# Low parts of the first product's weights and of the first q: VectorE in place of GpSimd

## The chip, the cores and the metric

The kernel runs on one core of a Trainium2 chip. The metric is the time of one execution on the device in microseconds (us). Five engines take part: TensorE (PE, with PEld for its weight loads), VectorE (DVE), ScalarE (ACT), GpSimd (POOL) and SyncE (SP), which issues most of the transfers.

## The reference

An attention with mixing across heads, and behind it two feed-forward blocks:

```
scores = einsum('bhij,hg->bgij', (q @ k^T) / sqrt(64), w_pre)
attn   = einsum('bhij,hg->bgij', softmax(scores), w_post)
x      = (attn @ v), heads side by side           # 1792 tokens x 768
x      = ((x @ w1) * (x @ w2)) @ w3 @ w_out       # 768 -> 1024 -> 1024 -> 768
out    = relu(x @ w_in)^2 @ w_out2                # 768 -> 2048 -> 768
```

There are 4 batches, 12 heads, 448 positions and a head width of 64. The weights arrive as 64-bit floats, two 32-bit words an element.

## The kernel before, in words

`w3 @ w_out` doesn't depend on x, so the kernel forms it first, once (`Prod34`): this is the first product. To multiply in 32-bit precision, each operand is split into a high part, in the reduced format that TensorE takes, and a low part, the difference to it; three matmuls (high-high, high-low, low-high) stand for one product (`mm3`, line 53).

The weights pass through `Weights` in 33 pieces: piece 0 and piece 2 are 256 columns wide, 16 pieces of w_out are 384 wide, and 15 pieces of w3 are 512 wide (7 of them in the first half, pieces 5, 8, ... 23; the last 8, pieces 25 to 32, belong to the second half). A piece goes through these steps:

- load on SyncE's queue into one of five `raw` buffers (line 68);
- `narrow` on ScalarE (line 80), which makes `y` from the upper words;
- `join` parts 0, 1, 2 on VectorE (lines 92, 94, 96), which put the 32-bit float `f` together;
- `high` on ScalarE (line 110), which writes the high part from `f`;
- `rest` on GpSimd (line 114), which writes the low part, `f` minus the high part.

The order on each engine is the order of the program, written by hand: nothing is reordered. `Prod34.stage(s)` issues, one after the other, the load of piece s+6, the narrow of s+4, then on VectorE join 1 of s+2, join 0 of s+3, join 2 of s+2, then the high part of s+2, and last the low part of s+1. `half0` runs 25 stages, with the matmuls of each stage's piece behind it, evacuates its sums (lines 194 and 195, columns split between ScalarE and VectorE) with two more stages between, and `half1` runs the remaining stages with the second half of the product.

Between the stages `prologue(i)` puts in the work that the attention needs first, by the table `PRO`: the loads of k and q of batch 0, the high part of q (`high_q`, line 313, on ScalarE for the first chunk n = 0) and its low part (`low_q`, line 318, on GpSimd for every n), the high parts of k (line 289, ScalarE) and their low parts (`low_k`, line 296, on VectorE for batch 0), the first score matmuls (`scores`, line 335) and their evacuation (`evac`, line 342, ScalarE). The score sums have two buffers. Chunk 0 has three groups of q, each of 480 columns and four heads; their steps are `split_q` at i = 5, 8 and 13. From i = 15 the steps of the attention proper are mixed in, and the feed-forward blocks follow, whose weights go through the same `Weights` class with its own stage order.

Of the kernel before, what the change touches and what calls it, by code (L numbers as in the profile page):

```python
# [14 lines left out]
ALU = mybir.AluOpType  # L15
# [18 lines left out]
def fused_kernel(ctx, tc, q, k, v, w_pre, w_post, w1, w2, w3t, wo, win, wo2, eye, out):  # L34
    nc = tc.nc
# [10 lines left out]
    def f32(ap):  # L46
        return ap.bitcast(F)
# [9 lines left out]
    class Weights:  # L57
# [51 lines left out]
        def high(self, i):  # L109
            nc.scalar.activation(self.out[i][0], self.ft[i], AF.Copy)  # L110

        def rest(self, i):
            if i in self.ft:
                nc.gpsimd.tensor_tensor(self.out[i][1], self.ft.pop(i), f32(self.out[i][0]), ALU.subtract)  # L114

    HC = DM // 2

    class Prod34:
# [29 lines left out]
        def stage(self, s):  # L148
            w = self.w
            ok = lambda i: 0 <= i < len(self.seq)  # L150
            if ok(s + 6):
                k, c, x, lo, hi, _ = self.seq[s + 6]
                src, n = (wo, HC) if k == "o" else (w3t, PW)
                w.load(s + 6, src[c, :, n * x + lo : n * x + hi], True)
            if ok(s + 4):
                w.narrow(s + 4)
            if ok(s + 2) and s > 0:
                w.join(s + 2, 1)
            if ok(s + 3):
                w.join(s + 3, 0)  # L160
                if s < 0:
                    w.join(s + 3, 1)
                    w.join(s + 3, 2)
            if ok(s + 2):
                if s >= 0:
                    if s == 0:
                        w.join(s + 2, 1)
                    w.join(s + 2, 2)
                k, c, x, lo, hi, _ = self.seq[s + 2]
                w.place(s + 2, tuple(t[:, lo:hi] for t in self.tile(k, c, x)))  # L170
                w.high(s + 2)
            if ok(s + 1):
                w.rest(s + 1)

        def product(self, acc, m, h, cs):
            for c in cs:
# [64 lines left out]
    class Attention:  # L241
# [73 lines left out]
        def low_q(self, n, g4):  # L315
            tl = self.ka.tile([128, 4 * IC], R, tag="ql", name=f"ql{n}_{g4}", bufs=3)
            tl = self.ql[n, g4] = tl[:, : 4 * CHUNKS[n % 4][1]]
            nc.gpsimd.tensor_tensor(tl, self.qraw.pop((n, g4)), f32(self.qh[n, g4]), ALU.subtract)

        def split_q(self, n, g4):  # L320
            self.high_q(n, g4)
# [558 lines left out]
```

## Time and profile before

| | |
|---|---|
| median of 3 runs | 1411.32 us (1411.06 to 1411.37) |
| the profiled execution | 1411.11 us, of which the span from first to last instruction 1409.2 us |
| TensorE busy in the span | 1375.7 us (98%) |
| VectorE, ScalarE, GpSimd busy | 771.5 us (55%), 643.0 us (46%), 509.5 us (36%) |
| mean granted TensorE clock | 0.994 of full speed |

The span is that of the trace; the time of the execution has 1.9 us around it. The shares are means over stages of different kinds: the first product and the prologue take the first 90 us or so, the attention and the feed-forward blocks the rest.

### The profile page before, as it was taken

The page shows a single profiled execution, that of the slowest core. Times are in us where ns is not written, and L with a number is a line of the kernel's source. Part 1 is how long each engine was busy: PE and PEld are TensorE (multiplying, and loading weights), DVE is VectorE, ACT ScalarE, POOL GpSimd, SP SyncE. Part 2 cuts the span into 40 slices and gives each one's busy share as a digit, 9 for nine tenths or more (in the row PEclk, how much of TensorE's full clock was granted, in tenths as well). Part 3 has the DMA queues.
Part 4 walks back from the last instruction along what each step waited for, and adds up shares of the span by engine and source line. Part 5 has one row for each costly group of instructions (what it writes and reads, how often), then busy time and mean ns, then how long its engine had stood idle before and what let it go on. Part 6 is the DMA issues. An engine that isn't in the chain of part 4 may idle for free.

```text
span 1409.2 us, 22743 instructions
## 1 busy us (share of the span) xinstructions
PE 1375.7 (98%) x8136; PEld 1191.6 (85%) x8136; DVE 771.5 (55%) x1320; ACT 643.0 (46%) x1394; POOL 509.5 (36%) x604
## 2 busy tenths in 40 slices
PE   6789999999999999999999999999999999999998
PEld 5678777777777777899999999999999999999998
DVE  8963444443444444645317963985454227944972
ACT  4456655666656655433323533543333224533530
POOL 4543563563455335322222322234222222222231
PEclk9899999999999999999999999999999999999999
DMA  7774463444455325533223442355443123433441
GB/s 217 226 229 149 151 186 127 154 165 151 148 165 161 127 97 170 154 107 101 64 61 101 125 124 78 106 179 185 117 112 104 53 79 101 128 109 80 126 140 59
DMA packets 95509, 183.69 MB, mean 130 GB/s; under 512 B 20581, under 2 KB 62053, under 8 KB 94949
## 3 DMA queue, kind: packets, MB, share of 16 engines
q1 hardware_dynamic: 89861, 178.82, 41.2%
q10 hardware_dynamic: 5536, 3.42, 0.8%
q8 instruction: 65, 1.06, 0.3%
q14 instruction: 47, 0.39, 0.1%
HBM read 129.52 MB, written 14.16 MB: 102 GB/s over the span
## 4 chain that ended last, share of the span: by engine, by line
PE 93%; DVE 3%; issue 2%; ACT 1%; DMA 1%; ACTq 0%; DVEq 0%
PE l L53 50%; PE sp L357 11%; PE tp L406 11%; PE y L53 8%; PE pv L448 6%; PE sc L335 5%; PE q L53 1%; DVE f L92 1%; DVE f L94 1%; DVE f L96 1%; PE e L53 1%; DMA kraw<-k 0%; DMA raw<-w3t 0%; ACT kt L289 0%; ACT y L80 0%
## 5 line engine op out<-in xcount | busy, mean ns | idle before, releaser
L114 POOL TENSOR_TENSOR wl<-f,wh 128x384 fp32r<-128x384 f32 (+1 forms) x176 | 196.1, 1118 | 501.4 <-ACT wh L110 480.8
L363 DVE TENSOR_REDUCE nm<-sp 120x1 f32<-120x448 f32 x180 | 112.3, 624 | 208.5 <-PE sp L357 205.8
L92 DVE TENSOR_SCALAR f<-y 128x384 int32<-128x384 int32 (+2 forms) x209 | 147.0, 703 | 88.1 <-POOL wl L114 83.1
L406 PEld LDWEIGHTS tp<-kwr,p 120*112 120x112 f32 (+1 forms) x1440 | 173.5, 176 | 24.6 <-issue 13.7
L406 PE MATMUL tp<-kwr,p 120*112 120x120 f32 (+1 forms) x1440 | 176.9, 266 | 0.0
L357 PE MATMUL sp<-r,kpre 120*120 120x448 f32 x360 | 173.4, 563 | 0.0
L342 ACT ACTIVATE s<-sc 120x448 f32<-120x448 f32 (+1 forms) x192 | 99.3, 542 | 108.6 <-PE sc L335 107.7
L96 DVE SCALAR_TENSOR_TENSOR f<-raw,f 128x384 int32<-128x384 int32 (+2 forms) x209 | 142.0, 679 | 6.1
L396 POOL TENSOR_SCALAR kwr<-kw,sm 120x120 f32<-120x120 f32 x180 | 106.6, 599 | 104.6 <-DVE sm L391 68.2
L94 DVE SCALAR_TENSOR_TENSOR f<-y,f 128x384 int32<-128x384 int32 (+2 forms) x209 | 139.4, 667 | 6.2
L53 PE MATMUL l<-bhh,wh 128*128 128x448 f32 x384 | 141.3, 368 | 0.0
L53 PE MATMUL l<-blh,wh 128*128 128x448 f32 x384 | 141.1, 368 | 0.0
L53 PE MATMUL l<-bhh,wl 128*128 128x448 f32 x384 | 139.4, 363 | 0.0
L110 ACT ACTIVATE wh<-f 128x384 fp32r<-128x384 f32 (+1 forms) x176 | 96.4, 548 | 85.1 <-DVE f L96 79.5
L371 ACT ACTIVATE p<-sp,nm 120x448 f32<-120x448 f32 x180 | 113.5, 631 | 30.4 <-PE tp L406 24.4
L335 PE MATMUL sc<-kt,qh 128*120 128x448 f32 (+1 forms) x192 | 119.1, 620 | 5.0 <-DVE kt L296 2.8
L80 ACT ACTIVATE y<-raw 128x384 f32<-128x384 f32 (+2 forms) x209 | 120.6, 577 | 7.3 <-DMA raw<-w3t 2.9
L448 PE MATMUL pv<-p,v 112*64 112x120 f32 (+1 forms) x1536 | 94.6, 266 | 0.8 <-DVE p L421 0.8
L724 ACT ACTIVATE r<-l 128x448 f32<-128x448 f32 x64 | 34.9, 546 | 116.6 <-PE l L53 116.6
L448 PEld LDWEIGHTS pv<-p,v 112*64 112x64 f32 x1536 | 74.2, 136 | 12.7 <-issue 1.2
L421 DVE COPY p<-tp 112x480 f32<-112x480 f32 (+1 forms) x90 | 58.9, 655 | 45.5 <-PE tp L406 45.3
L53 PEld LDWEIGHTS l<-bhh,wh 128*128 128x128 f32 x384 | 71.8, 187 | 7.2
(104 smaller groups left out, 2837.8 us busy)
## 6 DMA issues: line engine op xcount, KB each, us to landing
r<-s SPq DMA_DIRECT2D x172, 210.0 KB
raw<-w SPq DMA_DIRECT2D x64, 384.0 KB
raw<-win SPq DMA_DIRECT2D x64, 384.0 KB
raw<-wo SPq DMA_DIRECT2D x48, 512.0 KB
kraw<-k SPq DMA_DIRECT2D x24, 448.0 KB
qraw<-q SPq DMA_DIRECT2D x36, 240.0 KB
raw<-w3t SPq DMA_DIRECT2D x15, 512.0 KB
raw<-wo SPq DMA_DIRECT2D x16, 384.0 KB
```

The lines of the kernel that those rows point to most:

```text
L53: nc.tensor.matmul(acc, w, x, start=(first and i == 0 and j == 0), stop=(last and i == n - 1 and j == 2))
L80: nc.scalar.activation(y, self.raw[i][:, :, 1].bitcast(F), AF.Copy, scale=2.0**-112)
L92: nc.vector.tensor_scalar(fi, yi, 3, 0x7FFFFFFF, ALU.logical_shift_left, ALU.bitwise_and)
L94: nc.vector.scalar_tensor_tensor(fi, yi, -0x80000000, fi, ALU.bitwise_and, ALU.bitwise_or)
L96: nc.vector.scalar_tensor_tensor(fi, raw[:, :, 0], 29, fi, ALU.logical_shift_right, ALU.bitwise_or)
L114: nc.gpsimd.tensor_tensor(self.out[i][1], self.ft.pop(i), f32(self.out[i][0]), ALU.subtract)
L335: nc.tensor.matmul(sc[:ic], t[:, hh * ic : hh * ic + ic], self.kt[b, h // 2][:, h % 2], start=(i == 0), stop=(i == 1))
L357: nc.tensor.matmul(t[:kk], self.kpre[:kk, :kk], self.rt.pop(g)[:kk], start=True, stop=True)
L363: nc.vector.tensor_reduce(nm[:kk], self.sp[g][:kk], AX.X, ALU.max, negate=True)
L371: nc.scalar.activation(p[:kk], self.sp.pop(g)[:kk], AF.Exp, bias=self.nm.pop(g)[:kk], accum_out=self.sm[g // 2][:kk, g % 2 : g % 2 + 1],)
L406: nc.tensor.matmul(t[:, j, :, :cnt], p[:kk, j * JP : j * JP + JP], w[:kk, :, :cnt], start=True, stop=True)
L448: nc.tensor.matmul(t[64 * e : 64 * e + 64], self.v[b][:, j, g], self.p2[n][:, j, g, :ic], start=(j == 0), stop=(j == JC - 1),)
```

## The change

The low parts of all 33 pieces of the first product's weights, and the low parts of q in chunk 0, are computed on VectorE. In the stage the low part of piece s+1 is now issued ahead of the joins, where it was last. The feed-forward blocks keep GpSimd for theirs, as do the later q chunks.

```diff
-        def rest(self, i):
+        def rest(self, i, eng=nc.gpsimd):
             if i in self.ft:
-                nc.gpsimd.tensor_tensor(self.out[i][1], self.ft.pop(i), f32(self.out[i][0]), ALU.subtract)
+                eng.tensor_tensor(self.out[i][1], self.ft.pop(i), f32(self.out[i][0]), ALU.subtract)
...
             if ok(s + 4):
                 w.narrow(s + 4)
+            if ok(s + 1):
+                w.rest(s + 1, nc.vector)
             if ok(s + 2) and s > 0:
                 w.join(s + 2, 1)
...
                 w.high(s + 2)
-            if ok(s + 1):
-                w.rest(s + 1)
...
-            nc.gpsimd.tensor_tensor(tl, self.qraw.pop((n, g4)), f32(self.qh[n, g4]), ALU.subtract)
+            eng = nc.gpsimd if n else nc.vector
+            eng.tensor_tensor(tl, self.qraw.pop((n, g4)), f32(self.qh[n, g4]), ALU.subtract)
```

## Rows read from the trace of the kernel before

**Rows 1.** Page, first part: busy us of each engine, share, instructions.

```profile
PE 1375.7 (98%) x8136; PEld 1191.6 (85%) x8136; DVE 771.5 (55%) x1320; ACT 643.0 (46%) x1394; POOL 509.5 (36%) x604
```

**Rows 2.** Windows of three stretches: length; busy PE, PEld, DVE, ACT, POOL; clock; DMA.

```profile
0.00:50.00 50.00, 33.01 (x138) 29.57 (x139) 44.92 (x66) 23.36 (x44) 24.29 (x24) 0.90 0.73 217
50.00:91.00 41.00, 30.41 (x142) 26.97 (x141) 40.44 (x52) 23.79 (x42) 22.13 (x15) 0.91 0.78 253
91.00:1409.00 1318.00, 1312.32 (x7860) 1135.10 (x7858) 686.12 (x1204) 595.85 (x1309) 463.04 (x565) 1.00 0.40 123
```

**Rows 3.** Groups by shape, first 150 us: the joins; busy, mean ns, idle before.

```profile
L96 DVE SCALAR_TENSOR_TENSOR f<-raw,f 128x512 int32<-128x512 int32 x15 | 17.3, 1151 | 0.0
...
L94 DVE SCALAR_TENSOR_TENSOR f<-y,f 128x512 int32<-128x512 int32 x15 | 15.0, 1001 | 0.1
L92 DVE TENSOR_SCALAR f<-y 128x512 int32<-128x512 int32 x15 | 14.3, 951 | 0.2 <-ACT y L80 0.2
...
L94 DVE SCALAR_TENSOR_TENSOR f<-y,f 128x384 int32<-128x384 int32 x16 | 13.1, 817 | 0.1
...
L96 DVE SCALAR_TENSOR_TENSOR f<-raw,f 128x384 int32<-128x384 int32 x16 | 13.0, 813 | 0.0
...
L92 DVE TENSOR_SCALAR f<-y 128x384 int32<-128x384 int32 x16 | 6.9, 433 | 0.0
```

**Rows 4.** Timeline, 35 to 42 us: start, duration, engine, line; brackets: idle and releaser.

```profile
35.30 1.49 DVE L96 SCALAR_TENSOR_TENSOR f<-raw,f 128x512 int32<-128x512 int32 x1
...
36.90 0.64 ACT L110 ACTIVATE w3h<-f 128x512 fp32r<-128x512 f32 x1 [1.38 <-DVE f L96]
37.18 0.35 DVE L92 TENSOR_SCALAR f<-y 128x384 int32<-128x384 int32 x1
...
37.45 0.55 DVE L96 SCALAR_TENSOR_TENSOR f<-raw,f 128x384 int32<-128x384 int32 x1
37.61 1.51 POOL L114 TENSOR_TENSOR w3l<-f,w3h 128x512 fp32r<-128x512 f32 x1 [1.38 <-ACT w3h L110]
37.92 1.62 DVE L94 SCALAR_TENSOR_TENSOR f<-y,f 128x384 int32<-128x384 int32 x1
...
40.62 0.55 DVE L96 SCALAR_TENSOR_TENSOR f<-raw,f 128x384 int32<-128x384 int32 x1
...
41.20 0.53 ACT L110 ACTIVATE woh<-f 128x384 fp32r<-128x384 f32 x1 [1.33 <-DVE f L96]
```

**Rows 5.** Timeline, 4 to 88 us: single instructions of DVE, POOL and PE.

```profile
4.80 0.29 DVE L92 TENSOR_SCALAR f<-y 128x256 int32<-128x256 int32 x1 [4.80 <-ACT y L80]
...
48.63 1.49 DVE L96 SCALAR_TENSOR_TENSOR f<-raw,f 128x512 int32<-128x512 int32 x1
...
51.44 1.42 POOL L318 TENSOR_TENSOR ql<-qraw,qh 128x480 fp32r<-128x480 f32 x1 [1.87 <-ACT qh L313]
...
74.17 0.68 DVE L96 SCALAR_TENSOR_TENSOR f<-raw,f 128x512 int32<-128x512 int32 x1
74.77 0.68 DVE L94 SCALAR_TENSOR_TENSOR f<-y,f 128x512 int32<-128x512 int32 x1
75.37 0.41 DVE L92 TENSOR_SCALAR f<-y 128x512 int32<-128x512 int32 x1
75.71 0.68 DVE L96 SCALAR_TENSOR_TENSOR f<-raw,f 128x512 int32<-128x512 int32 x1
...
77.03 1.71 POOL L318 TENSOR_TENSOR ql<-qraw,qh 128x480 fp32r<-128x480 f32 x1 [3.06 <-ACT qh L313]
...
86.05 1.16 DVE L296 TENSOR_TENSOR kt<-kraw,kt 64x448 fp32r<-64x448 f32 x2
...
87.17 0.47 PE L335 MATMUL sc<-kt,qh 128*120 128x448 f32 x1 [0.42 <-ACT s L342]
```

**Rows 6.** Chain that ended last, in order of time: start, duration, what.

```profile
94.58 2.09 PE q L53 x12
```

## The prediction

> **What bounds the kernel now.** The page's first part names TensorE as the bound of the whole, busy 98% of the span [rows 1]. I then cut the span into windows, since a share is a mean. Behind 91 us TensorE is busy 1312.3 of 1318.0 us at a clock of 1.00. Ahead of it, where the changed lines run, VectorE is the full engine: 44.9 of the first 50 us, although its first instruction starts only at 4.80, and 40.4 of the next 41, while TensorE works 33.0 and 30.4 [rows 2, 5]. So the prologue lasts as long as VectorE's queue, and what is added to or taken from that queue up to the point where TensorE takes over moves the end one for one; later there are only 5.7 us of TensorE idle to absorb anything.
>
> That point is in the timeline: the scores of heads 4 and 5 start at 87.17, as the low part of their k, the pair of subtractions at 86.05, ends on VectorE [rows 5]. In the table `PRO` it stands behind stage 31, so behind every changed piece.
>
> Next, what VectorE's time consists of. Groups by shape give the joins means far above their undisturbed durations: the 512-wide join 2 takes 1151 ns in the mean but 0.68 at 75.71 [rows 3, 5]. The timeline says why: the join at 37.92 takes 1.62 us because GpSimd's low part runs from 37.61 to 39.12; the one at 37.45, just ahead of it, takes 0.55 [rows 4]. Whenever GpSimd has started first, the join waits until it has ended.
>
> **What the change removes.** The waiting of joins for GpSimd. By durations (mean minus undisturbed, 0.41, 0.68, 0.68 us for joins 0, 1, 2 at 512 wide [rows 5]; 0.35, 0.55, 0.55 at 384 [rows 4]): 15 × (0.54 + 0.32 + 0.47) + 16 × (0.08 + 0.27 + 0.26) = 29.8 us [rows 3], and about 0.8 for the two narrow pieces, 30.6. By elapsed time, from 4.80 to 87.21, 82.4 us: undisturbed joins follow each other by 0.27 and 0.47 us at 384 wide (37.18, 37.45, 37.92 [rows 4]) and by 0.60, 0.34 and again 0.60 at 512 (from 74.17 on [rows 5]), so 16 × 1.21 + 15 × 1.54 = 42.5; three pairs of k parts at 1.16 are 3.5; four copies, the narrow pieces and the preparation of the mixing weights are some 4.5 (an estimate by width). The rest, 31.9, is waiting. I take 31.0 and keep 30.6 to 31.9.
>
> **What it adds as work.** A 32-bit subtraction from two operands in SBUF is no row of VectorE at these widths; the k parts do just that, 448 wide, in 0.58 each [rows 5], which fits between the joins 1 and 2 at 0.47 (384) and 0.60 (512). So 16 × 0.47 + 15 × 0.60 + 2 × 0.34 = 17.2, and the first two groups of q, 480 wide, 2 × 0.57 = 1.1; the third comes behind the deciding point, where TensorE is the bound. Sum 18.3.
>
> If this were all, VectorE would gain 31.0 - 18.3 = 12.7 us. The Trainium skill's SBUF — State Buffer, section Who interferes with whom, says that GpSimd and a VectorE instruction with two SBUF inputs exclude each other for a whole instruction, the later one blocked. By that alone the sum would be 1411.1 - 12.7 = 1398.4; the trace agrees on the blocking (1.62 against 0.55 [rows 4]).
>
> **What it adds as waiting.** The low part of a piece needs `f` and the high part. In the new order join 2 of a piece is VectorE's last instruction of a stage, ScalarE's high part follows it, and the low part is VectorE's first instruction of the next stage. VectorE executes in order, so it stands still while ScalarE works, and the joins of the next two pieces, the next high part and the load into the freed buffer stand behind it. Before, the same wait was GpSimd's and cost VectorE nothing.
>
> Its price: from the start of join 2 at 384 wide, 0.55 to its end (40.62 to 41.17), 0.03 to ScalarE's start (41.20), 0.53 for the high part, and the hand-over to the next engine, 0.07 from 37.54 to GpSimd's 37.61 [rows 4]: 1.18, where the next join would have come after 0.47. Stall 0.71. At 512 wide: 1.49 until join 2 ends at 36.79 (0.68 undisturbed), 0.11 to 36.90, 0.64, 0.07, together 1.50 against 0.60. Stall 0.90. The hand-over to VectorE itself is bounded by nothing and by twice that, so 0.07 either way a piece; I take the row.
>
> Piece by piece, up to the deciding point:
> - 15 of the 384-wide pieces in full: 15 × 0.71 = 10.7. The first pieces are excepted: their low parts come behind a whole join of another piece. The preparation of the premix weights fills about 0.4 of one stall.
> - Eight 512-wide pieces in full (six of the first half, 25 and 32): 8 × 0.90 = 7.2.
> - Piece 20: the low part of q is issued first and waits for two ScalarE instructions. GpSimd waited for the same pair: join 2 from 48.63, end 50.12, GpSimd at 51.44 [rows 5], so 1.3 + 0.08 = 1.4.
> - Pieces 27 and 28: one copy of 0.47 stands between, 2 × 0.43 = 0.9. Piece 26 has two copies between, 30 and 31 a pair of k parts (1.16): nothing. If those covers were gone, 0.9 each.
> - Piece 29: q's second group waits for the high part, a k conversion and its own high part. Join 2 at 74.17 ends at 74.85, GpSimd started at 77.03 [rows 5]: 2.2 + 0.1 = 2.3.
>
> Sum 10.7 - 0.4 + 7.2 + 1.4 + 0.9 + 2.3 = 22.1 us.
>
> The VectorE page of the Trainium skill (VectorE: DVE Perf Modes, The DRAIN you can't avoid) says that semaphores between chained VectorE instructions cost nothing extra and that the number of instructions counts; this is measured inside one engine, and by it the 22.1 would be nothing and the time again 1398.4. No row here has the round trip over ScalarE on VectorE's queue, only on GpSimd's.
>
> **Costed at nothing.** The loads: a piece's buffer comes free later but stages lengthen by the same, so the lead in stages stays. TensorE: per piece of the first product it has 12 matmuls or none, 2.09 us at full clock [rows 6], two such per three pieces, whose VectorE time becomes (2 × 1.68 + 2.14) + 2 × 0.71 + 0.90 = 7.8. GpSimd is left idle there, and none of its other work starts earlier.
>
> **The sum.** -31.0 + 18.3 + 22.1 = +9.4 us, on the profiled execution's own 1411.1 (span and 1.9 around it; 0.2 under the median of the runs): 1420.5.
>
> **The rivals.**
> 1. *Faster: the round trip is hidden.* If ScalarE's high part were done when VectorE comes to the low part, blocking goes and only 18.3 comes: 1398.4. The turning point is a mean stall of 12.7 / 22.1 = 57% of mine, 0.41 and 0.52 us. Against it: ScalarE's instruction alone takes 0.53 and 0.64 [rows 4]. For it: VectorE's durations hold some tail that may overlap. Chance 0.07.
> 2. *No change: VectorE's delay isn't passed on whole.* TensorE's 5.7 idle us behind 91 [rows 2] could swallow some, leaving 1414.8; with shorter hand-overs too, 1411 to 1414. Against it: nothing suggests that idle waits for anything else than its own stages. Chance of ending within 0.2%: 0.06.
> 3. *Slower still: TensorE drops to its lower clock.* The prologue has 0.90 and 0.91 granted [rows 2]; more idle could put it at the lower of its two levels, 1.2 of 2.4 GHz, where 24 matmuls take 8.4 against VectorE's 7.8: 0.6 a step over seven steps, and 1.5 to 2 in the first TensorE-bound work behind the deciding point, 1426. Chance 0.12.
>
> **How the numbers follow.** The forecast has 0.75. Its own range: the hand-over gives ± 0.07 × 25 = 1.8, the blocking - 0.9 to + 0.4, so 1418 to 1423. The 8-in-10 range leaves out rival 1 and the far ends of 2 and 3: 1414.5 to 1424.5. A measurement of this kernel tells 0.2%, 2.8 us, from no change: slower 0.75 + 0.12 = 0.87, same 0.06, faster 0.07.
>
> **What would show it.** After: the joins' means in the prologue fall to their undisturbed values (512-wide join 0 to about 410 ns); VectorE, not GpSimd, has idle time ahead of line 114, ended by ScalarE's line 110, 0.6 to 0.9 us a piece and about 20 in all; VectorE's busy share of the first 90 us falls while the scores of heads 4 and 5 start near 96.5; from there everything is shifted by a constant. It would be wrong if that idle is under 13 us, or if the scores start late but the end doesn't.

## The result, and the profile after

The changed kernel takes 1419.44 us (median of 4 runs, 1418.92 to 1420.05), the kernel before 1411.28 beside it: a ratio of 1.0059, with a 95% interval of 1.0046 to 1.0072, so slower by 8.2 us. The forecast was 1420.5, with a range of 1414.5 to 1424.5.

The page's first part after the change, to be set beside [rows 1]:

```profile
PE 1376.7 (97%) x8136; PEld 1192.0 (84%) x8136; DVE 760.1 (54%) x1356; ACT 642.8 (45%) x1394; POOL 461.4 (33%) x568
```

36 instructions (33 low parts of weights, 3 of q) moved from GpSimd to VectorE, and yet VectorE is busy 11.4 us less: the time in which a join waited for GpSimd had counted as busy time. The windows over the same stretches as [rows 2], the last one to the end (columns: length; busy PE, PEld, DVE, ACT, POOL; clock; DMA share; GB/s):

```profile
0.00:50.00 50.00, 30.13 (x126) 25.72 (x127) 35.11 (x78) 21.36 (x40) 0.19 (x4) 0.93 0.67 200
50.00:91.00 41.00, 27.01 (x115) 24.20 (x115) 32.72 (x64) 20.83 (x37) 0.00 (x0) 0.84 0.68 222
91.00:1417.00 1326.00, 1319.53 (x7898) 1142.11 (x7896) 692.28 (x1216) 600.60 (x1318) 461.26 (x564) 1.00 0.40 124
```

VectorE went from 44.9 and 40.4 us of work to 35.1 and 32.7, but TensorE got less done in these 91 us, 57.1 us of work against 63.4. The engine that bounds the stretch has become less busy and the stretch longer: what grew is a wait. Groups by shape over the first 150 us show both sides of it (busy us, mean ns, idle before, releaser), the joins beside [rows 3]:

```profile
L114 DVE TENSOR_TENSOR w3l<-f,w3h 128x512 fp32r<-128x512 f32 x15 | 10.3, 690 | 6.0 <-ACT w3h L110 5.9
L96 DVE SCALAR_TENSOR_TENSOR f<-raw,f 128x512 int32<-128x512 int32 x15 | 10.3, 684 | 0.0
L94 DVE SCALAR_TENSOR_TENSOR f<-y,f 128x512 int32<-128x512 int32 x15 | 10.3, 684 | 0.0
...
L114 DVE TENSOR_TENSOR wol<-f,woh 128x384 fp32r<-128x384 f32 x16 | 8.9, 558 | 9.5 <-ACT woh L110 9.5
...
L92 DVE TENSOR_SCALAR f<-y 128x512 int32<-128x512 int32 x15 | 6.3, 420 | 0.0
```

The 512-wide joins fell from 951, 1001 and 1151 ns to 420, 684 and 684. In front of the low parts VectorE stands idle for 15.5 us, and ScalarE's high part ends 15.4 of them. One such wait at either width in the timeline (start, duration, engine, line; in brackets the idle time and what ended it):

```profile
21.41 0.55 DVE L96 SCALAR_TENSOR_TENSOR f<-raw,f 128x384 int32<-128x384 int32 x1
22.00 0.52 ACT L110 ACTIVATE woh<-f 128x384 fp32r<-128x384 f32 x1 [1.43 <-DVE f L96]
...
22.55 0.56 DVE L114 TENSOR_TENSOR wol<-f,woh 128x384 fp32r<-128x384 f32 x1 [0.59 <-ACT woh L110]
...
23.90 0.68 DVE L96 SCALAR_TENSOR_TENSOR f<-raw,f 128x512 int32<-128x512 int32 x1
24.68 0.63 ACT L110 ACTIVATE w3h<-f 128x512 fp32r<-128x512 f32 x1 [1.71 <-DVE f L96]
...
25.34 0.69 DVE L114 TENSOR_TENSOR w3l<-f,w3h 128x512 fp32r<-128x512 f32 x1 [0.76 <-ACT w3h L110]
```

From join 2 to the low part it is 1.14 and 1.44 us. And the place from which TensorE takes over, in the same columns:

```profile
93.62 0.69 DVE L114 TENSOR_TENSOR w3l<-f,w3h 128x512 fp32r<-128x512 f32 x1 [0.70 <-ACT w3h L110]
...
94.35 1.16 DVE L296 TENSOR_TENSOR kt<-kraw,kt 64x448 fp32r<-64x448 f32 x2
95.11 0.44 PE L336 MATMUL sc<-kt,qh 128*120 128x448 f32 x1 [0.32 <-DVE kt L296]
```

The scores of heads 4 and 5 start at 95.11 instead of 87.17 [rows 5], 7.9 us later; the span grew by 1417.1 - 1409.2 = 7.9. What happens behind this point has not changed its length, 1322.0 us in both; in the ten runs below it is 1321.6 to 1323.6 us.

### The profile page after: what moved, and what is told of

It is laid out like the page before. It is cut to its first block, busy times and chain, and to the rows that moved or that the text cites. A ratio compares the mean times of both kernels' runs of the same rounds, so it can differ in the third digit from the quotient of the medians.

```text
span 1417.1 us, 22708 instructions
## 1 busy us (share of the span) xinstructions
PE 1376.7 (97%) x8136; PEld 1192.0 (84%) x8136; DVE 760.1 (54%) x1356; ACT 642.8 (45%) x1394; POOL 461.4 (33%) x568
## 4 chain that ended last, share of the span: by engine, by line
PE 93%; DVE 3%; ACT 1%; issue 1%; DMA 1%; ACTq 0%; SPq 0%; DVEq 0%
PE l L53 50%; PE sp L358 11%; PE tp L407 10%; PE y L53 8%; PE pv L449 6%; PE sc L336 5%; PE q L53 2%; DVE f L94 1%; DVE f L96 1%; PE e L53 1%; ACT w3h L110 1%; ACT woh L110 0%; DVE f L92 0%; PE p L53 0%; DMA raw<-w3t 0%
## 5 line engine op out<-in xcount | busy, mean ns | idle before, releaser
L92 DVE TENSOR_SCALAR f<-y 128x384 int32<-128x384 int32 (+2 forms) x209 | 137.9, 660 | 87.9 <-POOL wl L114 83.1
L94 DVE SCALAR_TENSOR_TENSOR f<-y,f 128x384 int32<-128x384 int32 (+2 forms) x209 | 130.4, 624 | 6.1
L96 DVE SCALAR_TENSOR_TENSOR f<-raw,f 128x384 int32<-128x384 int32 (+2 forms) x209 | 130.0, 622 | 6.1
L319 POOL TENSOR_TENSOR ql<-qraw,qh 128x480 fp32r<-128x480 f32 (+1 forms) x45 | 51.0, 1134 | 109.2 <-DVE qh L311 109.2
```

Source lines behind the costliest of these rows:

```text
L92: nc.vector.tensor_scalar(fi, yi, 3, 0x7FFFFFFF, ALU.logical_shift_left, ALU.bitwise_and)
L94: nc.vector.scalar_tensor_tensor(fi, yi, -0x80000000, fi, ALU.bitwise_and, ALU.bitwise_or)
L96: nc.vector.scalar_tensor_tensor(fi, raw[:, :, 0], 29, fi, ALU.logical_shift_right, ALU.bitwise_or)
```

## The experiments

Ten kernels ran, all times medians beside the kernel before at 1411.3 on the same chip.

**The low parts on VectorE, at the end of the stage.** One block of the changed kernel moves, its operations and engine stay:

```diff
-            if ok(s + 1):
-                w.rest(s + 1, nc.vector)
             if ok(s + 2) and s > 0:
                 w.join(s + 2, 1)
...
                 w.high(s + 2)
+            if ok(s + 1):
+                w.rest(s + 1, nc.vector)
```

> The low parts stay on VectorE, but are issued at the end of the stage, behind join 2 of the next piece, where the high part has long been written. Theory (the loss is VectorE's wait for ScalarE's high part): of the sum's three terms the wait of the weights goes, only the two waits of q stay (1.4 and 2.3 us): -31.0 + 18.3 + 3.7 = -9.0 us against the kernel before, about 1402 us, range 1400 to 1405. Rival (the 33 subtractions themselves are the loss, wherever they stand): unchanged, about 1419 us.

Measured: 1403.99 us, a ratio of 0.9946 (0.9929 to 0.9963). The same 33 subtractions on the same engine are worth -7.3 us at one place of the stage and +8.2 at the other. VectorE's timeline of this run:

```profile
38.20 0.55 DVE L96 SCALAR_TENSOR_TENSOR f<-raw,f 128x384 int32<-128x384 int32 x1
38.67 0.68 DVE L114 TENSOR_TENSOR w3l<-f,w3h 128x512 fp32r<-128x512 f32 x1
39.27 0.55 DVE L94 SCALAR_TENSOR_TENSOR f<-y,f 128x384 int32<-128x384 int32 x1
...
64.42 0.43 DVE L92 TENSOR_SCALAR f<-y 128x512 int32<-128x512 int32 x1 [1.69 <-ACT y L80]
...
69.10 0.66 DVE L319 TENSOR_TENSOR ql<-qraw,qh 128x480 fp32r<-128x480 f32 x1 [3.05 <-ACT qh L313]
...
79.42 1.16 DVE L296 TENSOR_TENSOR kt<-kraw,kt 64x448 fp32r<-64x448 f32 x2
```

No low part of a weight has idle time ahead of it any more. The gain stayed 1.7 us under the 9.0 expected. Most of that is at the rows at 64.42 and 69.10: VectorE, now ahead, meets ScalarE's narrow step and waits longer for q. A smaller part lies at TensorE. Its window from the first scores of heads 0 and 1 to those of heads 4 and 5, in the columns of [rows 2], has no gap:

```profile
72.69:80.73 8.04, 8.04 (x33) 7.75 (x33) 7.75 (x14) 5.16 (x10) 0.00 (x0) 0.71 0.61 181
```

So the place from which TensorE is full has come forward to 72.69, and TensorE starts there at its lower clock, after 9 us without work: four score matmuls and twelve of the product take 1.82 and 3.47 us, the next ones 0.81 and 2.10. The scores of heads 4 and 5 start at 80.73, 0.7 us after the end of the k subtraction that they need (the first of the pair at 79.42, which takes 0.62), where it was 0.1 in the changed kernel.

**Between join 0 and join 2.** The same block behind `w.join(s + 3, 0)`.

> The low parts on VectorE between join 0 and join 2 of the stage: joins 1 and 0 (0.74 us at 384 wide, 0.94 at 512) lie over ScalarE's high part (wait 0.67 and 0.84 us in the changed kernel's trace). Theory: the wait is covered, as at the end of the stage, about 1402 us, no more than 1 us from that. Rival (the subtractions themselves): about 1419 us.

Measured: 1405.71 us (0.9961, 0.9946 to 0.9976). The wait is covered here too but for one low part (0.70 us), and the time is 1.7 us over the run before, more than the 1 us that was allowed. The traces put the difference into VectorE's idle time ahead of the scores of heads 4 and 5, 7.2 us here and 5.5 there: it waits longer for the narrow step (3.1 against 1.7) and shorter for q (3.4 against 3.8). Join 2, and with it the high part and the buffer for the next load, stands behind one more instruction here; whether the longer waits come from that wasn't separated.

**The wait without the work.** The low parts at the end of the stage, and a copy of one column of the high part, into a tile of its own (`probe`), at the front:

```diff
+            if ok(s + 1) and (s + 1) in w.ft:
+                nc.vector.tensor_copy(self.probe, f32(w.out[s + 1][0])[:, :1])
             if ok(s + 2) and s > 0:
                 w.join(s + 2, 1)
```

> The low parts at the end of the stage as in the run beside it, and at the front of the stage, where the changed kernel has them, a copy of one column of the high part on VectorE: the wait for ScalarE without the work. Theory: the wait comes back, about 18 us over the run with the low parts at the end, and 33 small copies of 0.06 to 0.1 us with it: 1420 to 1423 us. Rival (the place of the subtraction or its work counts, not the wait): 1402 to 1405 us, as without the copies.

Measured: 1410.46 us, between the two theories: only 6.5 us more than without the copies. The timeline says why:

```profile
22.06 0.68 DVE L96 SCALAR_TENSOR_TENSOR f<-raw,f 128x512 int32<-128x512 int32 x1
22.66 0.55 DVE L114 TENSOR_TENSOR wol<-f,woh 128x384 fp32r<-128x384 f32 x1
23.50 0.15 DVE L159 COPY probe<-w3h 128x1 f32<-128x1 f32 x1 [0.29 <-ACT w3h L110]
```

The copy still comes 1.44 us after join 2 started, but the low part of the piece before now stands between the two and fills most of it. The expectation had overlooked that the moved work itself is a cover, so this run doesn't decide.

**The wait without the work, with nothing between.** The same copy at the front, the low parts behind join 0:

> The low parts stand between join 0 and join 2, as in the run that gave 1405.7 us, and the copy of one column of the high part stands at the front of the stage, where now no other VectorE instruction lies between join 2 and it: the changed kernel's whole wait without its work at that place. Theory: the changed kernel's time and 33 small copies at 0.07 us: 1419.4 + 2.3 = 1421.7 us, range 1420 to 1423. Rival (the place of the work counts, not the wait): 1405.7 + 2.3 = 1408 us.

Measured: 1421.43 us (1.0074, 1.0059 to 1.0089), 15.7 us over the same order without the copies. The timeline:

```profile
21.71 0.55 DVE L96 SCALAR_TENSOR_TENSOR f<-raw,f 128x384 int32<-128x384 int32 x1
22.85 0.15 DVE L159 COPY probe<-woh 128x1 f32<-128x1 f32 x1 [0.59 <-ACT woh L110]
...
25.70 0.15 DVE L159 COPY probe<-w3h 128x1 f32<-128x1 f32 x1 [0.76 <-ACT w3h L110]
```

The copies stand idle 0.59 and 0.76 us, to the hundredth as the low parts in the changed kernel, and 15.4 us in all, as they do. The 15.7 us aren't this wait alone: a copy adds a step of 0.08 us (22.85 to 22.93 in the same timeline), some 2.6 for 33, and VectorE's other waits shrink from 6.5 to 4.0. One column is enough to bring the loss back: it is the wait.

**Every low part twice**, in a row, at the changed kernel's place:

> The changed kernel with every low part of the first product's weights written twice in a row on VectorE: no further wait, 17.2 us more work on VectorE. Theory (VectorE's queue sets the end of the prologue, one for one): 1419.4 + 17.2 = 1436.6 us, less up to 1 for what the two pairs of k parts cover. Rival (part of the work hides behind another engine): less than 1430 us.

Measured: 1440.08 us, 20.6 more than the changed kernel; next to none of the added work was hidden, and it was dearer than expected. In the timeline the second writing starts 0.60 us behind the first, where a join follows by 0.47:

```profile
22.86 0.56 DVE L115 TENSOR_TENSOR wol<-f,woh 128x384 fp32r<-128x384 f32 x1 [0.59 <-ACT woh L110]
23.46 0.56 DVE L116 TENSOR_TENSOR wol<-f,woh 128x384 fp32r<-128x384 f32 x1
23.93 0.55 DVE L94 SCALAR_TENSOR_TENSOR f<-y,f 128x384 int32<-128x384 int32 x1
```

At 0.60 for the 384-wide and 0.73 (as read at 19.65 and 20.38 there) for the 512-wide, 16 × 0.60 + 15 × 0.73 is 20.6 us, and about 0.9 for the narrow ones; against that one early wait shrank by 0.6 (1.21 to 0.59).

**GpSimd's blocking alone.** The low parts at the end of the stage on VectorE, and the same subtraction on GpSimd into a buffer that nobody reads (shown against the kernel with the low parts at the end of the stage):

```diff
             if ok(s + 1):
+                if (s + 1) in w.ft:
+                    f, h = w.ft[s + 1], w.out[s + 1][0]
+                    z = self.p.tile([128, PW], R, tag="dup", name=f"dup{s}", bufs=1)
+                    nc.gpsimd.tensor_tensor(z[:, : f.shape[1]], f, f32(h), ALU.subtract)
                 w.rest(s + 1, nc.vector)
```

> The low parts on VectorE at the end of the stage (1404.0 us), and GpSimd computes the same 33 subtractions once more into a buffer of its own that nobody reads: its share of the blocking without its part in the result. Theory (the first term of the sum: GpSimd holds VectorE up by 31 us): 1404 + 31, less the 5 us or so of VectorE's other waits that this hides: 1430 us, range 1425 to 1436. Rival (joins were slow for another reason than GpSimd, so its work costs nothing): 1404 us.

Measured: 1430.11 us (1.0134, 1.0117 to 1.0151), 26.1 over the run without it, as expected. The groups of this run:

```profile
L96 DVE SCALAR_TENSOR_TENSOR f<-raw,f 128x384 int32<-128x384 int32 x16 | 14.4, 898 | 0.0
...
L94 DVE SCALAR_TENSOR_TENSOR f<-y,f 128x512 int32<-128x512 int32 x15 | 12.7, 844 | 0.1
L92 DVE TENSOR_SCALAR f<-y 128x512 int32<-128x512 int32 x15 | 12.2, 813 | 0.0
L92 DVE TENSOR_SCALAR f<-y 128x384 int32<-128x384 int32 x16 | 12.1, 753 | 0.9 <-POOL dup L176 0.9
...
L96 DVE SCALAR_TENSOR_TENSOR f<-raw,f 128x512 int32<-128x512 int32 x15 | 10.2, 680 | 0.0
```

Which join pays is a matter of which comes up while GpSimd works: join 0 at both widths, the 512-wide join 1 and the 384-wide join 2, while the 512-wide join 2 stays at 680 ns. GpSimd could also hold VectorE up through a buffer `f` that it still reads; that is 0.9 us of idle time.

**No low parts of the weights at all**, on the kernel before (TensorE reads the high part where the low one stood):

> The kernel before without the 33 low parts of the weights on any engine; TensorE reads the high part in their place, so the number of matmuls stays. Theory: VectorE's 31 us of waiting for GpSimd go, but by 1400 us the loads, ScalarE's queue and TensorE come into view (the best kernel so far still gains only 10.6), so 1385 to 1398 us, and the joins run at their undisturbed 0.41, 0.68, 0.68 us. Rival (joins slow for another reason): 1411 us and the joins' means as before.

Measured: 1394.26 us (0.9880, 0.9865 to 0.9894). The groups:

```profile
L94 DVE SCALAR_TENSOR_TENSOR f<-y,f 128x512 int32<-128x512 int32 x15 | 11.2, 744 | 0.1
L96 DVE SCALAR_TENSOR_TENSOR f<-raw,f 128x512 int32<-128x512 int32 x15 | 10.2, 683 | 0.0
...
L92 DVE TENSOR_SCALAR f<-y 128x512 int32<-128x512 int32 x15 | 6.6, 438 | 10.8 <-ACT y L80 10.6
```

The joins are at or near their undisturbed durations (join 1's mean, 744 ns, holds one join of 1.60 us beside GpSimd's low part of q), and VectorE now waits for the narrow step (10.8 us at this width): of the 31 us estimated, 17 arrive at the end.

**The two halves of the change.** The weights alone (q back on GpSimd), and q alone (the weights as before):

> The changed kernel with q's low parts back on GpSimd, so the weights' part of the change alone. Two waits of VectorE get shorter (1.25 to 0.76 and 2.03 to 0.76 us) and two subtractions of 0.57 go, but GpSimd blocks a join or a low part for about 1.2 us each time: theory 1418 to 1420 us, the same as the whole change. Rival (q's two waits are what makes it slower): 1411 to 1414 us.

> The kernel before with q's low parts alone on VectorE. VectorE waits for ScalarE at two places (1.4 and 2.2 us), does 1.1 us more, and gets 1.4 and 1.5 us of blocking back: theory 1412 to 1413 us. Rival (q's waits make the change slower): 1416 us or more.

Measured: 1418.73 us (1.0053, 1.0036 to 1.0070) and 1412.42 us (1.0009, 1.0000 to 1.0018). The weights make 7.4 of the 8.2 us, q about 1.

**q's low parts one step later**, with the weights' at the end of the stage:

```diff
-            for kind in ("low_k", "high_k", "split_q"):
+            for kind in ("low_k", "high_k", "high_q", "low_q"):
```

In the table `PRO` the steps are (5, 8, 13) for `high_q` and (6, 9, 13) for `low_q`.

> Low parts of the weights on VectorE at the end of the stage (1404.0 us), and the low parts of q's first two groups one prologue step behind their high parts, so that VectorE comes to them when ScalarE is done. Theory: VectorE's two waits there (0.79 and 3.05 us) go, 1404.0 - 3.8 = 1400.2 us, less what the wait for the narrow step ahead of them (1.69 us) grows by: 1400 to 1403. Rival (the loads or ScalarE's queue now set the prologue's end): 1404 us.

Measured: 1400.68 us (0.9926, 0.9911 to 0.9941), 10.6 us under the kernel before and 18.8 under the changed one: the best of all that computes everything. Its chain ahead of the first scores has turned to loads:

```profile
53.11 7.29 DMA raw<-w3t
60.40 0.02 issue
60.41 6.99 DMA kraw<-k
...
69.41 1.85 PE sc L336 x4
```

## Why the prediction was right

**VectorE's queue sets the prologue's end, one for one.** Right: VectorE needed from 4.73 until 95.51 in the changed kernel, 90.8 us, against 82.4 [rows 5]; the scores and the span moved by 7.9, and the scores start at 95.11 where 96.5 was forecast. Writing the low parts twice, and waiting with the copies, passed through nearly whole. In the other direction the rule ends where TensorE is full: with the low parts at the end of the stage that is from 72.69 on.

**The blocking goes, 31.0 us.** Right in kind and about right in size, though no run measures it alone: the joins are at their undisturbed means, and giving GpSimd its subtractions back without any use for them cost 26.1 us in a kernel that has 5.5 us of other waits to hide some. The rule of the Trainium skill on the port that both engines share (SBUF — State Buffer, Who interferes with whom) agrees with the rows, 1.62 us beside GpSimd against 0.55 [rows 4]; what takes the place of the blocking is no part of it. The prediction quotes it for instructions with two inputs in SBUF, but join 0, with one, was held up as well (951 ns before, 420 after).

**The work, 18.3 us.** A low part takes 0.48 and 0.61 us until the next instruction starts (22.55 to 23.03, 25.34 to 25.95), 0.47 and 0.60 were estimated; over all pieces that is 0.3 us.

**The wait for ScalarE, 22.1 us.** The deciding term, and the one that was somewhat oversized. The idle time ahead of the low parts is 15.4 us for the weights and 3.3 for q; an instruction that doesn't wait would have started 0.08 us before the end of the one ahead, which adds some 2 for about 26 waits: 20.8. A full wait is 1.14 - 0.47 = 0.67 and 1.44 - 0.60 = 0.84 us where 0.71 and 0.90 were taken, which over 15 and 8 pieces is 1.1 us; the two waits of q and the two half-covered pieces came out a few tenths shorter, and one early piece (1.21 us idle at 12.50, since ScalarE had waited for a load until 11.37) longer. That piece makes up by chance what the other 384-wide ones fell short of: together they are 10.7 us, as forecast. So the sum at VectorE is -31.0 + 18.6 + 20.8 = +8.4 instead of +9.4, and measured were 90.8 - 82.4 = 8.4. The other 0.4 lies in the hand-over at the deciding point: there the scores need the first of the two k subtractions alone; in the kernel before they had been held by ScalarE's evacuation, as the row's releaser says [rows 5], and not by the pair's end, as the prediction read it. From the timeline of the kernel before:

```profile
85.33 0.69 DVE L96 SCALAR_TENSOR_TENSOR f<-raw,f 128x512 int32<-128x512 int32 x1
...
86.06 0.63 ACT L110 ACTIVATE w3h<-f 128x512 fp32r<-128x512 f32 x1 [2.12 <-DVE f L96]
86.59 0.96 ACT L342 ACTIVATE s<-sc 120x448 f32<-120x448 f32 x2
```

The evacuation stands behind a high part that had waited for VectorE's join 2, so the path led through VectorE's queue all the same.

**The rivals.** The hidden round trip (1398.4) didn't happen, but another order comes within 2.3 us of it: with the low parts where ScalarE is already done, 1404.0, and with q's treated likewise 1400.7. TensorE's idle time behind the deciding point took up nothing of the delay: 1322.0 us to the end before and after. That semaphores cost nothing extra (the Trainium skill's VectorE: DVE Perf Modes, The DRAIN you can't avoid) doesn't carry over to a wait for another engine that has yet to do its part: 15.7 us for 33 copies of one column. TensorE's granted clock did go lower, 0.84 against 0.91 from 50 to 91 us, but TensorE had the time: at 95.11 it had stood idle for 0.32 us, until VectorE's subtraction ended. Behind the deciding point the clock was 1.00.

## What to carry to other kernels

Moving work from a slow engine to the busy one can pay even if it adds instructions, when the slow one had been holding the busy one up; but an engine that executes in order must not meet the moved instruction where its input is being made. Look for the producer in the timeline, and place the consumer behind at least as much other work as the round trip lasts; here 1.1 to 1.4 us a piece, and one instruction's place in the stage decided between -7.3 and +8.2 us. Busy time that falls while the stretch grows is the sign of it.

## What the runs showed of the hardware that wasn't expected

Two subtractions in a row into the same tile follow each other by 0.60 us at 384 wide and 0.73 at 512, where an instruction on another tile follows by 0.47 and 0.60; the 0.13 us, 31 times, are 4.0 us, and with the early wait that shrank they leave the 3.4 us by which the doubled low parts were dearer than counted. Whether the shared tile causes it was not tested. And GpSimd's blocking falls on whichever join comes next: with the 33 subtractions on GpSimd once more, but in another rhythm against VectorE's, join 0's mean at 384 wide rose to 753 ns from 433 [rows 3], and the 512-wide join 2's fell to 680 from 1151.
